# Attention plus mixer on one core: one token tile of two batches is kept and multiplied with the next batch's tile as a seven-product pair

## The chip, the cores and the metric

The kernel runs on one core of one Trainium2 chip. The metric is the device time of one execution in microseconds (us). Engines are named as in the profile: PE is TensorE (matrix products; PEld its weight loads), DVE is VectorE, ACT is ScalarE, POOL is GpSimd, and SP is the queue that issues most transfers.

## The reference, cut to what matters

Eight batches, 12 heads, 448 tokens, 64 elements a head:

```
scores = q @ k^T / sqrt(64) - log(448)
x  = sigmoid(scores) @ v               # per head, heads side by side: [8, 448, 768]
u  = x + (relu(x^T @ w_tok1) @ w_tok2)^T
out = u + relu(u @ w_ch1) @ w_ch2      # w_ch1 768 x 1536, w_ch2 1536 x 768
```

The last line is the part that the change touches: for each batch, `h2 = relu(u @ w_ch1)` has 448 tokens of 1536 values, and the output is `h2 @ w_ch2` plus `u`, in fp32.

## The kernel before, in words

The work is a pipeline written out by hand: each engine runs its instructions in the order of the program, and waits by semaphores. Token tiles of a batch are 0, 1 and 2 (128 tokens each) and a last one of 64.

Batches 3 to 7 run in `steady(b, u)`, three cycles (u = 0, 1, 2) a batch. A batch b brings 21 units of attention scores (`score`, L187 on PE, a sigmoid on ACT at L194), 6, 6 and 9 in the three cycles; `av` multiplies the sigmoids of the cycle before by v (L218), casts the result on DVE (L227) and sends it through a transposing transfer (`xtrans_dma`). `tok_tail` and `tok1` are the first product of the token mixer (L277, L296) with ReLUs on ACT (L310); `ytrans` is the second (L316), added to x on DVE (L326). After the second cycle's `ytrans` a copy (L339) and the transfer `un` (L343) put u of batch b - 1 into token order.

The third cycle ends with `sevens(b - 1)`, the product with w_ch1 for batch b - 1 by seven products in place of eight (Strassen's scheme in Winograd's form; L514), in the order "1ab 2a 2b 1c 6ab 5ab 2c 6c 5c 7ab 7c 3ab 4ab 3c 4c". ACT copies products 1, 6 and 5 out of PSUM into buffers `parts` (L535); DVE adds later ones to them (L544, L547). Its token sums (`token_sums`, L457) are made on DVE earlier in the third cycle.

The product with w_ch2, here called the output product, runs two batches behind: in batch b it is that of lot b - 2. Tiles 0 and 1 of the lot form a pair of rows for `ch2_seven`: seven products, numbered 1 to 7, each 6 matmuls of 384 columns, with weights that are sums of parts of the two tiles (`sums`, L801, DVE). The products accumulate on three chains: 1, 6, 7, 4 on bank X in this order, 2 on Y, 5 and 3 on Z (Y and Z are the same bank, one after the other). After each product, DVE adds what the bank holds to the output (L841), and the next product of that chain has to wait for this read. After products 3 and 4 the two tiles' outputs are stored (`store`, L621, two transfers on SP).

Two products can run side by side in quarters of the array (`two_jobs`, L861, six steps of four 64x64 matmuls in each of two halves). Between the halves stands `turn_over`, a copy of one column by DVE (L852, `turned`), for which PE waits. In cycle 0 the pair (1, 2) runs like this, then 6 and 5 as plain products (L814); in cycle 1 the pair (7, 3), then 4. The plain products stand between `tok1` and `ytrans`. Cycle 2 does the 64-token tile (`last_split`, L669) and then tile 2 alone: `ch2_pair`, 7 of 12 blocks in quarters (L387), the other 5 as 10 plain matmuls (L650) right before `sevens`, with an add on DVE for each half (L607).

Three copies of q and k into pair order for the next batch (`rel_k`, `rel_q`, L129) are made on DVE: one after cycle 0's `ytrans`, two in cycle 1 before `tok_tail`, three after cycle 1's `ytrans`; the transposing transfers `tr_k` and `tr_q` (L142) follow on SP. GpSimd issues the loads of later batches once `tr_q` has landed.

Buffers: output tiles 0 and 1 share a ring of four buffers, `parts`, with ACT's copies; a buffer is free again when its store has landed. Tile 2 has a buffer of its own (`outs`). `h2` has one buffer, `un` two.

Of the kernel before, what the change touches and what calls it, by code (L numbers as in the profile page):

```python
# [9 lines left out]
FP16 = mybir.dt.float16  # L10
FP32 = mybir.dt.float32
# [10 lines left out]
NJ = 7  # L22
NP = 64
NU = 3
# [6 lines left out]
def kernel(  # L31
# [11 lines left out]
    nc = tc.nc  # L43
# [6 lines left out]
    NCB = CC // 128  # L50
# [10 lines left out]
    pa = ctx.enter_context(tc.tile_pool(name="pa", bufs=2))  # L61
# [286 lines left out]
    h2 = {}  # L348
# [110 lines left out]
    def ch1_seven(b, banks):  # L459
# [300 lines left out]
    class ch2_seven:  # L760

        CHAIN = {1: "X", 6: "X", 7: "X", 4: "X", 2: "Y", 5: "Z", 3: "Z"}

        def __init__(self, rows, sides, X, Y, Z, at_end=True):
# [3 lines left out]
            hid = pa.tile(  # L768
                [128, 3, NCB // 2, 128], FP16, tag=tag, bufs=bufs, name=f"hid_{b}"
            )  # L770
            self.held = {n: hid[:, at, :, :] for at, n in enumerate((5, 6, 7))}
# [62 lines left out]
        def end(self, n):  # L834
            row, half = {1: (0, 0), 2: (0, 0), 6: (0, 1), 3: (0, 1)}.get(n, (1, int(n != 4)))
            b, t = self.rows[row]
            if (b, t) not in outs:
                out_tile(b, t)
            o = outs[b, t][:, DH * half : DH * half + DH].rearrange("s (u d) -> s u d", d=128)
            opens = n in (1, 6, 5, 4)  # L840
            nc.vector.tensor_tensor(  # L841
                out=o,
                in0=un[b][:, :, half, t, :] if opens else o,
                in1=self.ps[self.CHAIN[n]][:, 0:DH].rearrange("s (u d) -> s u d", d=128),
                op=ADD,
            )
            if n in (3, 4):
                store(b, t)

    def turn_over(ps):  # L850

        nc.vector.tensor_copy(out=turned[:, :], in_=ps[:, 0:1])  # L852
# [448 lines left out]
    def score(n=1):  # L1301
        for _ in range(n):
            qk(*next(scores))

    def steady(b, u):

        lot, before, ahead = b - 2, divmod(NU * b + u - 1, NU), divmod(NU * b + u - 2, NU)
# [2 lines left out]
        def run(steps, n):  # L1310
            for f in steps[:n]:
                f()
            del steps[:n]

        at_bank[0] = X
        if u < 2:
# [31 lines left out]
            at_bank[0] = Y  # L1348
            tok_tail(*ahead)
            tok1(*ahead, with_scores=True)  # L1350
            for n in ((6, 5), (4,))[u]:
                seven.plain(n)
        else:
            ps = [bank([128, 512], FP32, f"c2_{lot}_3_{r}") for r in range(2)]
            steps, end = last_split(lot, ps)
# [138 lines left out]
```

## Time and profile before

| what | us |
|---|---|
| median of three runs | 342.08 (341.51 to 342.49) |
| profiled execution, its own time | 341.39 |
| its span on the core | 339.6 |
| one batch of `steady` (each of 3 to 7) | 38.3 |
| PE busy | 332.2 (98%) |
| DVE busy | 234.9 (69%) |
| ACT busy | 213.0 (63%) |

How to read it: the columns of a timeline are start in us from the span's start, duration in us, engine, line of the kernel, operation, output and input, and a count; in square brackets stands the idle time before it and what ended that. Rows merge neighbours of one kind, and matmuls overlap, so the time that PE spends on some is read from the start of one row to the start of the next. The share of time that an engine is busy is an average over a batch whose three cycles differ.

### The profile page before, as it was taken

The page shows a single profiled execution, that of the slowest core. Times are in us where ns is not written, and L with a number is a line of the kernel's source. Part 1 is how long each engine was busy: PE and PEld are TensorE (multiplying, and loading weights), DVE is VectorE, ACT ScalarE, POOL GpSimd, SP SyncE. Part 2 cuts the span into 40 slices and gives each one's busy share as a digit, 9 for nine tenths or more (in the row PEclk, how much of TensorE's full clock was granted, in tenths as well). Part 3 has the DMA queues.
Part 4 walks back from the last instruction along what each step waited for, and adds up shares of the span by engine and source line. Part 5 has one row for each costly group of instructions (what it writes and reads, how often), then busy time and mean ns, then how long its engine had stood idle before and what let it go on. Part 6 is the DMA issues. An engine that isn't in the chain of part 4 may idle for free.

```text
span 339.6 us, 10285 instructions
## 1 busy us (share of the span) xinstructions
PE 332.2 (98%) x4423; PEld 242.5 (71%) x4423; DVE 234.9 (69%) x484; ACT 213.0 (63%) x272; POOL 58.7 (17%) x102
## 2 busy tenths in 40 slices
PE   7999999999999999999999999999999999999994
PEld 4555565555796679866896679866896679769852
DVE  2277366678998973877768773878758654876882
ACT  3997657388647895578647895578647795314200
POOL 8981550050031000220032002020010000000000
PEclk9999999999999999999999999999999999999999
DMA  7999999999999999998999899988995293028007
GB/s 119 173 174 195 206 205 204 163 175 237 169 187 189 140 168 211 185 142 161 204 145 172 138 206 175 206 117 134 196 175 93 56 193 73 2 56 185 4 11 197
DMA packets 104381, 52.17 MB, mean 154 GB/s; under 512 B 76432, under 2 KB 101264, under 8 KB 104336
## 3 DMA queue, kind: packets, MB, share of 16 engines
q1 hardware_dynamic: 78704, 29.11, 47.8%
q0 software_dynamic: 25168, 21.50, 42.1%
q10 hardware_dynamic: 464, 0.92, 1.0%
q8 instruction: 34, 0.56, 0.7%
q14 instruction: 11, 0.09, 0.1%
HBM read 43.45 MB, written 11.01 MB: 160 GB/s over the span
## 4 chain that ended last, share of the span: by engine, by line
PE 86%; DMA 5%; POOL 4%; ACT 2%; issue 1%; DVE 0%; ACTq 0%; POOLq 0%
PE c_ab L514 14%; PE c L814 10%; PE qk L187 9%; PE c_c L514 8%; PE xa L218 7%; PE c L861 6%; PE tk L296 5%; PE yt L316 5%; PE c L387 4%; DMA c<-in_moe_w_ch_dram 4%; PE c L584 4%; PE c L364 3%; PE c L669 3%; PE c L650 2%; ACT att L194 2%; DMA raw_v<-in_v_dram 2%
## 5 line engine op out<-in xcount | busy, mean ns | idle before, releaser
L194 ACT ACTIVATE att<-qk,att_bias 128x896 f16<-128x896 f32 x168 | 156.0, 1012 | 38.6 <-PE qk L187 37.6
L187 PE MATMUL qk<-tr_q,tr_k 64*64 64x448 f16 x672 | 61.3, 360 | 0.3 <-ACT att L194 0.2
L514 PEld LDWEIGHTS <-c 128*128 128x128 f16 x504 | 48.4, 98 | 1.1 <-issue 0.3
L218 PE MATMUL xa<-att,raw_v 64*64 64x448 f16 x644 | 40.7, 349 | 0.0
L187 PEld LDWEIGHTS <-tr_k 64*64 64x64 f16 x672 | 25.2, 105 | 19.0 <-issue 11.9
L514 PEld LDWEIGHTS <-sum 128*128 128x128 f16 x378 | 36.3, 98 | 0.0
L227 DVE CAST xu<-xa 128x448 f16<-128x448 f32 x40 | 23.1, 619 | 18.8 <-PE xa L218 18.4
L535 ACT ACTIVATE pt_ab<-c_ab 128x896 f32<-128x896 f32 x21 | 19.2, 917 | 20.6 <-PE c_ab L514 20.6
L218 PEld LDWEIGHTS <-raw_v 64*64 64x64 f16 x672 | 22.0, 107 | 8.3 <-issue 0.4
L861 PE MATMUL c<-c,h 64*64 64x384 f16 x360 | 24.6, 322 | 0.0
L1127 POOL COPY gate<-tr_q 128x2 f16<-128x2 f16 x6 | 1.6, 275 | 121.7 <-DMA tr_q<-rel_q 121.7
L326 DVE TENSOR_TENSOR xu<-xu,yt 128x448 f16<-128x448 f16 x38 | 21.7, 613 | 0.0
L537 ACT ACTIVATE h<-c_ab 128x896 f16<-128x896 f32 x7 | 6.4, 917 | 24.4 <-PE c_ab L514 24.4
L296 PE MATMUL tk<-xn,w 128*128 128x256 f16 x156 | 21.2, 274 | 0.1
L544 DVE TENSOR_TENSOR h<-pt_ab,c_ab 128x896 f16<-128x896 f32 x14 | 15.2, 1084 | 8.6 <-PE c_ab L514 8.6
L544 DVE TENSOR_TENSOR h<-pt_c,c_c 128x448 f16<-128x448 f32 x21 | 12.9, 614 | 11.7 <-PE c_c L514 11.6
L316 PE MATMUL yt<-w,h 128*128 128x448 f16 x88 | 20.3, 353 | 0.0
L841 DVE TENSOR_TENSOR o<-un,c 128x384 f32<-128x384 f16 x32 | 17.4, 550 | 4.0 <-PE c L814 4.0
L310 ACT ACTIVATE h<-tk 128x256 f16<-128x256 f32 x42 | 14.2, 406 | 9.5 <-PE tk L296 9.5
L814 PEld LDWEIGHTS <-hid 128*128 128x128 f16 x132 | 12.9, 98 | 8.0
L514 PE MATMUL c_ab<-diffs,c 128*128 128x224 f16 x168 | 18.4, 259 | 0.0
L296 PEld LDWEIGHTS <-w 128*128 128x128 f16 x156 | 13.6, 98 | 5.7 <-issue 2.4
(134 smaller groups left out, 572.1 us busy)
## 6 DMA issues: line engine op xcount, KB each, us to landing
out_dram<-o SPq DMA_DIRECT2D x41, 192.0 KB, 3.2
c<-in_moe_w_ch_dram POOLq DMA_DIRECT2D x4, 1152.0 KB, 16.1
raw_k<-in_k_dram POOLq DMA_DIRECT2D x10, 336.0 KB, 6.9
raw_q<-in_q_dram POOLq DMA_DIRECT2D x10, 336.0 KB, 5.7
raw_v<-in_v_dram POOLq DMA_DIRECT2D x10, 336.0 KB, 8.8
out_dram<-o SPq DMA_DIRECT2D x15, 96.0 KB, 2.4
raw_q<-in_q_dram POOLq DMA_DIRECT2D x12, 112.0 KB, 5.1
raw_k<-in_k_dram POOLq DMA_DIRECT2D x12, 112.0 KB, 5.4
```

Of the source, the lines that this page charges most:

```text
L187: nc.tensor.matmul(out=ps[64 * g : 64 * g + 64, hi, 0:S], lhsT=tr[b, "k"][64 * hi : 64 * hi + 64, u, j, 64 * g : 64 * g + 64], rhs=tr[b, " ...
L194: nc.scalar.activation(out=att[b, u, j][:, :, :], in_=ps[:, :, 0:S], func=SIGMOID, bias=bias_t[:, :], scale=att_scale,)
L218: nc.tensor.matmul(out=ps[g][64 * hi : 64 * hi + 64, 0:S], lhsT=raw[b, "v"][64 * g : 64 * g + 64, u, hi, j, :], rhs=att[b, u, j][64 * g : ...
L227: nc.vector.tensor_copy(out=xu(b)[:, u, g, 0:S], in_=ps[g][:, 0:S])
L296: nc.tensor.matmul(out=ps[tcb], lhsT=w1[rows, t, cols], rhs=xn[b, u][rows, :, t, :], start=(t == 0 and not with_scores), stop=(t == (2 if ...
L316: nc.tensor.matmul(out=ps[:, 0:S], lhsT=h1[b, u][:, tcb, g, :], rhs=w2[:, tcb, :, :], start=(tcb == 0), stop=(tcb == 1),)
L326: nc.vector.tensor_tensor(out=x, in0=x, in1=ps[:, 0:S], op=ADD)
L514: nc.tensor.matmul(out=ps[:, g, p, :], lhsT=weights[n][:, d, 128 * cb : 128 * cb + 128], rhs=moving[n][:, d, :], start=(n in (1, 5, 2) and ...
L535: nc.scalar.activation(out=shaped(part[:, :, :]), in_=ps, func=COPYF)
L544: nc.vector.tensor_tensor(out=shaped(dst), in0=shaped(parts[gs, which]), in1=ps, op=ADD)
L814: nc.tensor.matmul(out=ps[:, 0:DH], lhsT=self.weights[n][:, k, :], rhs=self.moving[n][:, k, :], start=(n in (1, 2, 5) and k == 0), stop=(k ...
L861: nc.tensor.matmul(out=ps[m : m + 64, 0:DH], lhsT=lhsT(n)[part, m : m + 64], rhs=rhs(n)[part, :], start=(opens and turn == 0 and n == 0), ...
```

## The change

In batches 4 and 6 tile 2 of the lot (lots 2 and 4) is not multiplied. Instead its `h2` columns are copied to a buffer `late` (which takes the place of `outs`) and its part of `un` to `un_late`, both on DVE. In the batch that follows (5 and 7) it forms a pair with tile 2 of the next lot (3 and 5), and seven products do both: (1, 2) in quarters, then 6, 5, 7, 3, 4 as plain products before `sevens`. The four sums of weights overwrite columns of `h2` that are no longer needed. The outputs of tile 2 of lots 2 to 5 now come from `parts`.

In batches 4 and 6 the products of the pair of tiles 0 and 1 are placed anew: (1, 2) and 6 in the first cycle, (5, 7) and no plain product in the second, (3, 4) in quarters at the start of the third. So both of their stores are issued in the third cycle. The order of `rel_k`, `rel_q` and the transfers around them is as before. Batch 3 and the end of the kernel are as before.

```diff
+    LATE_TILE = {4: 2, 6: 4}
+    PAIRED = {b + 1: lot for b, lot in LATE_TILE.items()}
+    un_late = {}
...
-        tag, bufs = ("outs", 1) if t == 2 else ("parts", 4)
+        late = b in LATE_TILE.values() or b - 1 in LATE_TILE.values()
+        tag, bufs = ("outs", 1) if t == 2 and not late else ("parts", 4)
...
+    def late_pair(lot):
+        free = h2[lot]
+        return ch2_seven(
+            [(PAIRED[lot + 2], 2), (lot, 2)],
+            [h2[PAIRED[lot + 2], "late"], free[:, :, 256:384]],
+            X,
+            X + 1,
+            X + 1,
+            at_end=False,
+            held={
+                5: free[:, LOW, 0:128],
+                6: free[:, HIGH, 0:128],
+                7: free[:, LOW, 128:256],
+                3: free[:, HIGH, 128:256],
+            },
+        )
...
-            turn0, turn, turn1, end = two_jobs([seven.job(n) for n in ((1, 2), (7, 3))[u]])
+            pair = ((1, 2), (5, 7) if b in LATE_TILE else (7, 3))[u]
+            turn0, turn, turn1, end = two_jobs([seven.job(n) for n in pair])
...
-            for n in ((6, 5), (4,))[u]:
+            for n in ((6,), ())[u] if b in LATE_TILE else ((6, 5), (4,))[u]:
                 seven.plain(n)
+        elif b in LATE_TILE:
+            turn0, turn, turn1, end = two_jobs([sevenfold[lot].job(n) for n in (3, 4)])
+            score(2)
+            run(turn0, 6)
+            turn()
+            at_bank[0] = Y
+            av(*before, 0, 2)
+            score()
+            run(turn1, 4)
+            score()
+            run(turn1, 2)
+            end()
+            av(*before, 2, 5)
+            score()
+            av(*before, 5, NJ)
+            xtrans_dma(*before)
+            at_bank[0] = X
+            ps = [bank([128, 512], FP32, f"c2_{lot}_3_{r}") for r in range(2)]
+            steps, end = last_split(lot, ps)
+            run(steps, 4)
+            score()
+            token_sums(b - 1)
+            run(steps, 3)
+            score()
+            run(steps, 3)
+            score()
+            run(steps, 2)
+            end()
+            late = pa.tile([128, NCB, 128], FP16, tag="outs", bufs=1, name=f"late_{lot}")
+            nc.vector.tensor_copy(out=late[:, :, :], in_=h2[lot][:, :, 256:384])
...
+            nc.vector.tensor_copy(out=un_late[lot][:, :, :, :], in_=un[lot][:, :, :, 2, :])
+            h2[lot, "late"] = late
+            at_bank[0] = Y
+            tok_tail(*ahead)
+            score()
+            tok1(*ahead, with_scores=True)
+            sevens(b - 1)
         else:
...
-            turn0, turn1, rest = ch2_pair(lot, u, 7, loose=True)
+            if b in PAIRED:
+                both = late_pair(lot)
+                turn0, turn, turn1, end = two_jobs([both.job(n) for n in (1, 2)])
+                rest = lambda: [both.plain(n) for n in (6, 5, 7, 3, 4)]
+            else:
+                turn0, turn1, rest = ch2_pair(lot, u, 7, loose=True)
+                turn, end = lambda: turn_over(turn_bank[0]), lambda: None
             run(turn0, 3)
             score()
             run(turn0, 4)
-            turn_over(turn_bank[0])
+            turn()
             av(*before, 5, NJ)
             xtrans_dma(*before)
             send()
+            if b in PAIRED:
+                both.sums(0, 2)
             token_sums(b - 1)
             score()
             run(turn1, 2)
             score()
             run(turn1, 5)
+            end()
+            if b in PAIRED:
+                both.sums(2, 4)
```

More of the change, by code (lines that the diff above doesn't have):

```diff
@@ L762, with __init__ @@
         CHAIN = {1: "X", 6: "X", 7: "X", 4: "X", 2: "Y", 5: "Z", 3: "Z"}
-        def __init__(self, rows, sides, X, Y, Z, at_end=True):
+        def __init__(self, rows, sides, X, Y, Z, at_end=True, held=None):
             self.rows, self.ps, self.banks = rows, {}, {"X": X, "Y": Y, "Z": Z}
@@ L767, in __init__ @@
             tag, bufs = ("tr_k", 2) if at_end else ("diffs", 1)
[L768 to L771, printed above, removed]
+            self.held = held
+            if not held:
+                hid = pa.tile(
+                    [128, 3, NCB // 2, 128], FP16, tag=tag, bufs=bufs, name=f"hid_{b}"
+                )
+                self.held = {n: hid[:, at, :, :] for at, n in enumerate((5, 6, 7))}
             if at_end:
@@ L840, in end @@
             opens = n in (1, 6, 5, 4)
+            u = un_late[b][:, :, half, :] if t == 2 and b in un_late else un[b][:, :, half, t, :]
             nc.vector.tensor_tensor(
                 out=o,
-                in0=un[b][:, :, half, t, :] if opens else o,
+                in0=u if opens else o,
                 in1=self.ps[self.CHAIN[n]][:, 0:DH].rearrange("s (u d) -> s u d", d=128),
@@ L1350, in steady @@
             tok1(*ahead, with_scores=True)
-            for n in ((6, 5), (4,))[u]:
+            for n in ((6,), ())[u] if b in LATE_TILE else ((6, 5), (4,))[u]:
                 seven.plain(n)
+        elif b in LATE_TILE:
[28 more added lines that the diff above has]
+            nc.vector.tensor_copy(out=late[:, :, :], in_=h2[lot][:, :, 256:384])
+            un_late[lot] = pa.tile(
+                [128, NU, 2, 128], FP16, tag="un_late", bufs=1, name=f"un_late_{lot}"
+            )
+            nc.vector.tensor_copy(out=un_late[lot][:, :, :, :], in_=un[lot][:, :, :, 2, :])
[5 more added lines that the diff above has]
+            sevens(b - 1)
         else:
```

1 line of the change is left out of this document (added).

## The prediction

> **What bounds the kernel now.** I read the busy shares, then busy time by batch, then the timelines of one batch on each engine. In the busy shares and in the stretches of batches 3 to 7 (columns: stretch, sum, TensorE, weight loads, VectorE, ScalarE, GpSimd, granted clock, DMA share, GB/s):
>
> ```profile
> PE 332.2 (98%) x4423; PEld 242.5 (71%) x4423; DVE 234.9 (69%) x484; ACT 213.0 (63%) x272; POOL 58.7 (17%) x102
> 140.48:178.79 38.31, 38.31 (x568) 30.11 (x564) 27.86 (x60) 26.87 (x35) 4.53 (x8) 1.00 0.98 168
> ```
>
> TensorE never pauses inside a batch, and all five batches take 38.3 us, so any TensorE time removed counts, unless another engine is then late. How late the others already are stands in the timelines of batch 4, TensorE first (start, duration; 6 matmuls of 384 columns start 0.163 us apart: 153.85 to 154.83):
>
> ```profile
> 153.85 1.14 PE L814 MATMUL c<-hsum_b,h 128*128 128x384 f16 x6
> 154.83 0.92 PE L316 MATMUL yt<-w,h 128*128 128x448 f16 x4
> 155.68 0.57 PE L187 MATMUL qk<-tr_q,tr_k 64*64 64x448 f16 x8
> ...
> 164.03 1.79 PE L650 MATMUL c<-c,h 128*128 128x384 f16 x10
> 165.66 1.31 PE L514 MATMUL c_ab<-xu,c 128*128 128x224 f16 x12
> ```
>
> The third cycle starts at 155.68, the channel products (L514) at 165.66. Around the end of the second cycle:
>
> ```profile
> 154.26 0.69 ACT L310 ACTIVATE h<-tk 128x256 f16<-128x256 f32 x2
> 155.00 0.30 PEld L316 LDWEIGHTS <-h 128*128 128x128 f16 x3 [0.18 <-ACT h L310]
> ```
>
> The second weight load of `yt` starts 0.05 us after ScalarE's second ReLU ends (154.95): ScalarE is already the last to arrive. VectorE in the third cycle:
>
> ```profile
> 155.50 1.14 DVE L326 TENSOR_TENSOR xu<-xu,yt 128x448 f16<-128x448 f16 x2
> 156.68 0.23 DVE L339 COPY xu<-xu 128x192 f16<-128x192 f16 x1
> 156.82 1.66 DVE L129 COPY rel_q<-raw_q 128x896 f16<-128x896 f16 x3
> ...
> 161.28 0.16 DVE L852 COPY turned<-c 128x1 f32<-128x1 f32 x1 [1.60 <-PE c L387]
> 161.51 1.16 DVE L227 CAST xu<-xa 128x448 f16<-128x448 f32 x2
> 162.81 0.92 DVE L457 TENSOR_TENSOR diffs<-xu 128x672 f16<-128x672 f16 x2
> ```
>
> It opens the cycle with 3 us of queued work and reaches `turned` (TensorE waits for it between the halves of a quad pair) idle; until 164.82 it does casts and token sums. The SP queue:
>
> ```profile
> 154.75 1.18 SPq L621 DMA_DIRECT2D out_dram<-o  x2
> 156.02 4.07 SPq L142 DMA_TRANSPOSE tr_k<-rel_k  x1
> 160.18 1.19 SPq L621 DMA_DIRECT2D out_dram<-o  x2
> 161.47 4.39 SPq L343 DMA_TRANSPOSE un<-xu  x1
> 165.99 3.17 SPq L142 DMA_TRANSPOSE tr_q<-rel_q  x1
> ```
>
> Each big transpose holds SP for 3 to 4.4 us; the second tile's store, ready at 155.6 (its last add on VectorE), went out at 160.18.
>
> **The change part by part.** Batches 4 and 6 keep, 5 and 7 pair. I work on batch 4's clock; batch 5's is 38.31 later. The products shrink by 6 matmuls a pair, 0.98 us; without any wait the two pairs would give -1.95.
>
> *Keeping batch, first cycle.* Product 5 goes: 6 x 0.163 = -0.98, in full, for the ReLUs there end at 146.76 and `yt` would start at 146.80. Its add (0.55 on VectorE) was hidden.
>
> *Second cycle.* Product 4 stood between `tok1` and `yt`, another -0.98. But `yt` now follows `tok1` at once and needs the ReLUs, queued behind six back-to-back sigmoids (148.90 to 154.26). Between 0 (ScalarE sets `yt`) and -0.98; the 0.05 us above says 0. So the third cycle starts 0.98 early, at 154.70.
>
> *Third cycle.* 14 quad steps and 10 plain matmuls go, 12 quad steps (products 3 and 4) come: -0.32 and -1.63. New is the place of `turned`: early in the cycle, behind the `yt` adds, L339 and three `rel_q` copies, which end at 158.48 - 0.98 = 157.50; with its 0.16 TensorE goes on at 157.72. TensorE gets there after 0.40 (two scores), 6 x 0.162, two `av` steps 0.38 and a score 0.19, at 156.64: a wait of 1.08, with everything behind it on TensorE. The split of the last tile reuses the banks that two adds must first read: 0.1 more. From 157.72 to the ninth score are 12 quad steps at 0.163, six at 0.163 of products 3 and 4, five `av` at 0.19, five scores at 0.19, `tok_tail` 0.15 and that 0.1: 5.1, so 162.8 against 163.0 before. ScalarE, idle during the wait, follows within 0.9 a score. Then 10 plain matmuls fewer: L514 starts at 163.83, -1.83 where the work alone says -3.90.
>
> *The two copies.* 1536 and 768 half-precision elements: 1.55 us by L129 (0.61 for 896), 1.1 by L547 (0.43 for 896); I take the copy row, 1.55. They end near 166.2, where VectorE's first combine is due at 167.96 - 1.83 = 166.1; the bank that this reads is needed again only 5.2 us after L514's start, 169.0. Cost nothing; without that cover 1.1 to 1.6.
>
> *Stores moved past transposes.* The stores of tiles 0 and 1 now both follow products 3 and 4, so on SP they come after `tr_k`, `un` and `tr_q`. From `rel_k` done (155.12 - 0.98, so 154.2): 4.07 + 4.39 + 3.17 and gaps of 0.1 make 166.1; the four halves go out 0.6 apart. Stores landed 3.1 to 4.4 us after issue in this stretch: tile 0 at 169.9 to 171.1, tile 1 at 171.0 to 172.3. Their buffers (`parts`) are those that ScalarE fills after channel products 6ab and 5ab; 6ab ends at 163.83 + 4.03 = 167.86 (before, those stores had landed 6 us earlier). ScalarE waits until about 170.5. TensorE meets it at 7ab and again at 7c, which comes 8.05 after L514's start and needs 6c's sums read: after tile 0's landing 1.2 to tile 1's, fills of 0.92 (5ab) and 0.55 (6c) and 0.1, so 173.3 instead of 171.9: 0.8 to 2.1, I take 1.4. `xn`, behind the stores, issues near 168.6 and is needed at 183. The loads that GpSimd gates on `tr_q` start some 3 us sooner. Keeping batch: -1.83 + 1.4 = -0.43.
>
> The Trainium skill ("DMA: Bandwidth & Descriptors", section "Issuing engines are not separate DMA queues") says that the time a sequencer spends on initiating a DMA is usually small relative to the DMA itself. Here `un` holds SP for 4.39 us of its 6.5 to landing, so the measurement decides; by the rule the stores would leave when their adds are done, this term would be 0, and the sum would be that of the second rival.
>
> *Pairing batch, third cycle.* Two quad steps fewer (-0.32), but the ninth score hangs on ScalarE's nine sigmoids (156.17 to 164.71, no gap), so 0.07 of it counts. `tok1` ends at 163.96. Five plain products, 30 matmuls, 4.88, stand where 10 (1.63) stood. Product 6 accumulates onto product 1's bank, which the first add must have read. On VectorE that add comes after `turned` (0.16 earlier, 161.12), the casts, two sums of 0.53 each and all four token sums: 164.82 + 1.05 - 0.16 = 165.7, read by 166.25. TensorE waits from 163.96 to 166.3: 2.35. Product 6 then 5 end at 168.25; product 7 needs the bank that product 6's add has read, behind the two later sums, at 168.5: 0.2 more. Product 4 ends at 171.42, against 165.66: +5.76 (work alone +2.93). Who waits: the channel products and all later.
>
> The paired tiles' buffers are awaited by 6ab and 6c. In batch 7 no loads run and the stores land in time. In batch 5, tile 2's store of before took 5.5 us beside the k and v loads, in batch 4 4.3; the kept tile's second half, on SP near 210.9, would land at 215.2 to 216.4. L514 starts at 209.3, 7c is due at 217.35 and waits for that landing, two fills of 0.92, one of 0.55 and 0.1: 0.4 to 1.6 late, 1.0.
>
> *Sum.* 2 x (5.76 - 0.43) + 1.0 = +11.7. The profiled execution took 341.39 (span 339.6), so 353.1; the median of the runs, 342.08, stands 0.69 above it: 353.7.
>
> **Rivals.** (1) *The work alone decides.* TensorE has been 98% busy and no row of before shows it waiting for VectorE in a batch: the time falls by 0.98 a pair, to 340.1. That holds if product 1's add is read by 163.96 and the other waits stay under a microsecond a pair. Against it: VectorE's rows fill 161.28 to 164.82 even without the two sums.
> (2) *The stores land in time.* If SP gives them out before `tr_q`, or its transposes are shorter with `un` issued sooner (the shortest of all was 3.64), nothing waits on `parts`: 2 x (5.76 - 1.83) = +7.9, 349.9. For it: the margin is 2 us in a chain of three transposes; against: SP issues in program order.
> (3) *The clock drops.* A pause of 2.35 us is longer than any wait of TensorE listed in this trace (1.2), and the granted clock is 1.00 in every batch. If it halved over the next three products, 18 x 0.163 = 2.9 a pair more: 359.6. The Trainium skill ("TensorE: Matmul & The Clock Gate", section "Why this matters for your kernels") warns of idle gaps above about 3 us; this one would stay under it, and no trace here shows a gap of that length.
> (4) *The stores land later still*, as batch 5's did (5.5) in both keeping batches: 2 x 1.1 and 0.6 more, 356.5.
>
> **How the numbers follow.** The forecast has 0.53, the work alone 0.05, stores in time 0.22, the clock 0.06, later stores 0.12; 0.02 is for a change under 0.3%. A measurement of this kernel tells about 0.3%, 1 us, from no change. Predicted 353.7; the range 349.3 to 357.0 takes in the forecast, in-time and later stores, 0.87, and leaves out the work alone, the clock and no change. Faster 0.05, within 0.3% 0.02, slower 0.93.
>
> **What would show it.** In the profile after: batches 4 and 6 near 37.9 us, batch 5 near 45, batch 7 near 44; TensorE's busy share near 94%; waits on TensorE for the add of `o` before the pair's product 6 (2.3 us, twice) and for `turned` in the keeping batches' third cycle (1.1, twice); weight loads of `yt` ended by the ReLU in the keeping batches' second cycle (0.9); ScalarE's `pt_ab` released by a store (2 to 3). I am wrong if product 6 starts right behind `tok1`, or if the keeping batches gain more than 2 us.

## The result, and the profile after

| | before | after |
|---|---|---|
| median of 6 runs each | 341.3 us (340.53 to 342.49) | 357.67 us (354.55 to 360.24) |
| profiled execution, its own time | 341.39 | 354.55 |
| its span | 339.6 | 352.8 |

The ratio is 1.0465 (95% interval 1.0431 to 1.05; it leaves out the slowest run, 360.24, which counts as slow): the change costs some 16 us by the medians and 13.2 us by the two profiled executions. The forecast was 353.7 with a range of 349.3 to 357.0, so the direction was right and the size too small. The profiled execution is the fastest of the runs of the changed kernel; what the others lost more is taken up below.

The busy shares of the changed kernel, and its busy time in batches 4, 5, 6 and 7 (columns as before: stretch, sum, TensorE, weight loads, VectorE, ScalarE, GpSimd, granted clock with 1.00 for full speed, DMA share, GB/s):

```profile
PE 333.2 (94%) x4387; PEld 239.1 (68%) x4387; DVE 243.7 (69%) x502; ACT 212.3 (60%) x272; POOL 58.1 (16%) x102
```

```profile
138.69:176.30 37.61, 35.41 (x536) 26.81 (x536) 27.75 (x60) 26.77 (x35) 4.58 (x8) 1.00 1.06 164
176.30:224.62 48.32, 43.47 (x579) 32.02 (x578) 32.17 (x68) 26.62 (x35) 4.52 (x8) 0.96 0.90 161
224.62:263.06 38.44, 35.40 (x535) 26.81 (x534) 27.67 (x59) 26.77 (x35) 3.20 (x6) 1.00 0.89 140
263.06:306.65 43.59, 41.52 (x579) 31.43 (x578) 28.75 (x62) 26.84 (x35) 0.00 (x0) 1.00 0.46 78
```

TensorE went from 98% to 94% with about the same busy time: 36 matmul records fewer, and pauses in every one of the four batches. Against 38.31 each, batch 4 gains 0.70, batch 5 loses 10.01, batch 6 loses 0.13 and batch 7 loses 5.28: together +14.7. The part ahead of batch 4 was 1.6 shorter (138.69 against 140.28; no instruction there was changed by the edit's text, and later runs gave 138.88 to 142.59), the rest differs by less than 0.1. So the loss lies in the pairing batches, and batch 5 loses twice what batch 7 does with the same instructions on TensorE. Batch 5 is also the only one of the four whose granted clock is not 1.00. Of the signs that the prediction named, batches 4 and 6 near 37.9 (38.0 on average), batch 7 near 44 (43.59) and the busy share near 94% came; batch 5, expected near 45, did not.

The waits of TensorE are in its timeline. The first two rows are of batch 4, the next three of batch 5, the last of batch 7 (in brackets the pause and what ended it):

```profile
152.17 1.02 PE L316 MATMUL yt<-w,h 128*128 128x448 f16 x4 [0.70 <-ACT h L310]
...
155.95 0.35 PE L869 MATMUL c<-hsum_b,h 64*64 64x384 f16 x2 [0.72 <-DVE turned L860]
...
202.25 3.27 PE L821 MATMUL c<-hsum_a,h 128*128 128x384 f16 x12 [2.28 <-DVE o L849]
...
208.80 1.31 PE L514 MATMUL c_ab<-xu,c 128*128 128x224 f16 x12
...
218.40 1.31 PE L514 MATMUL c_ab<-diffs,c 128*128 128x224 f16 x12 [2.54 <-ACT pt_ab L535]
...
288.81 2.11 PE L821 MATMUL c<-hsum_a,h 128*128 128x384 f16 x12 [2.07 <-DVE o L849]
```

The pauses that the forecast named are there: `yt` for the second ReLU, `turned` in the keeping batch, and product 6 of the pair for the first add of `o`, 2.28 and 2.07 us. What it did not have is in the durations. The first twelve matmuls after the pause took 3.27 in batch 5 and 2.11 in batch 7. From product 6 to L514 it is 208.80 - 202.25 = 6.55 in batch 5 and, in batch 7, whose L514 starts at 293.72, 4.91. The granted clock says why (busy time in four short stretches, the first three of batch 5, the last of batch 7):

```profile
202.20:204.00 1.80, 1.75 (x8) 0.94 (x8) 1.77 (x4) 0.00 (x0) 0.00 (x0) 0.73 1.01 182
204.00:206.00 2.00, 2.00 (x8) 0.96 (x7) 0.64 (x2) 0.00 (x0) 0.00 (x0) 0.50 1.16 216
206.00:208.00 2.00, 2.00 (x13) 1.14 (x12) 0.66 (x2) 0.00 (x0) 0.18 (x1) 0.89 1.07 197
288.80:291.00 2.20, 2.19 (x14) 1.30 (x14) 1.99 (x5) 0.00 (x0) 0.00 (x0) 1.00 0.34 69
```

After the pause of 2.28 the clock was 0.50 for about 3.4 us (in slices of 0.2 us it lies below 1.00 from 203.0 to 206.6, in the first and the last only in part); after the pause of 2.07, in this execution, it stayed at 1.00, and so it did after the pause of 2.54 further down.

The second thing in batch 5 is the pause of 2.54 at 7ab (218.40), behind a `pt_ab` that ScalarE could not write. ScalarE's timeline and SP's, both of batch 5, and then the transfers issued from 204 to 218 (KB each, median us from issue to landing):

```profile
217.43 1.73 ACT L535 ACTIVATE pt_ab<-c_ab 128x896 f32<-128x896 f32 x2 [5.01 <-DMA out_dram<-o]
```

```profile
197.47 4.75 SPq L343 DMA_TRANSPOSE un<-xu  x1
202.33 3.26 SPq L142 DMA_TRANSPOSE tr_q<-rel_q  x1
205.69 1.28 SPq L243 DMA_TRANSPOSE xn<-xu  x1
...
208.61 3.31 SPq L626 DMA_DIRECT2D out_dram<-o  x4
```

```profile
out_dram<-o SPq DMA_DIRECT2D x4, 192.0 KB, 7.7
raw_k<-in_k_dram POOLq DMA_DIRECT2D x2, 336.0 KB, 6.8
raw_v<-in_v_dram POOLq DMA_DIRECT2D x2, 336.0 KB, 10.4
```

The pair's four stores leave SP from 208.61 on, in the same moment as GpSimd's loads of `k` and `v` (from 208.25), and land 7.7 us after issue, where the stores of the keeping batches took 3.0 and 3.2.

### The profile page after: what moved, and what is told of

Read it like the earlier page. It is cut to its first block, busy times and chain, and to the rows that moved or that the text cites. A ratio compares the mean times of both kernels' runs of the same rounds, so it can differ in the third digit from the quotient of the medians.

```text
span 352.8 us, 10233 instructions
## 1 busy us (share of the span) xinstructions
PE 333.2 (94%) x4387; PEld 239.1 (68%) x4387; DVE 243.7 (69%) x502; ACT 212.3 (60%) x272; POOL 58.1 (16%) x102
## 4 chain that ended last, share of the span: by engine, by line
PE 74%; ACT 10%; DVE 6%; DMA 6%; issue 2%; SPq 0%; ACTq 0%; DVEq 0%
PE c L821 12%; PE c_ab L514 11%; ACT att L194 9%; PE qk L187 8%; PE xa L218 6%; PE c_c L514 6%; PE c L869 6%; PE yt L316 5%; DMA out_dram<-o 5%; PE tk L296 4%; PE c L589 3%; PE c L364 3%; PE c L674 2%; DMA first_q<-in_q_dram 1%; PE c L899 1%
## 5 line engine op out<-in xcount | busy, mean ns | idle before, releaser
L187 PE MATMUL qk<-tr_q,tr_k 64*64 64x448 f16 x672 | 59.3, 357 | 0.7 <-ACT att L194 0.2
L514 PEld LDWEIGHTS <-c 128*128 128x128 f16 x504 | 48.4, 98 | 6.3 <-issue 5.7
L514 PEld LDWEIGHTS <-sum 128*128 128x128 f16 x378 | 36.3, 98 | 0.0
L849 DVE TENSOR_TENSOR o<-un,c 128x384 f32<-128x384 f16 x36 | 19.7, 551 | 5.6 <-PE c L821 5.6
L821 PEld LDWEIGHTS <-h 128*128 128x128 f16 x120 | 12.2, 103 | 13.2 <-issue 6.5
L849 DVE TENSOR_TENSOR o<-o,c 128x384 f32<-128x384 f32 x30 | 16.3, 552 | 7.0 <-PE c L821 3.7
L514 PE MATMUL c_ab<-diffs,c 128*128 128x224 f16 x168 | 18.4, 259 | 2.5 <-ACT pt_ab L535 2.5
```

Of the source, the lines that this page charges most:

```text
L187: nc.tensor.matmul(out=ps[64 * g : 64 * g + 64, hi, 0:S], lhsT=tr[b, "k"][64 * hi : 64 * hi + 64, u, j, 64 * g : 64 * g + 64], rhs=tr[b, " ...
L514: nc.tensor.matmul(out=ps[:, g, p, :], lhsT=weights[n][:, d, 128 * cb : 128 * cb + 128], rhs=moving[n][:, d, :], start=(n in (1, 5, 2) and ...
L821: nc.tensor.matmul(out=ps[:, 0:DH], lhsT=self.weights[n][:, k, :], rhs=self.moving[n][:, k, :], start=(n in (1, 2, 5) and k == 0), stop=(k ...
L849: nc.vector.tensor_tensor(out=o, in0=u if opens else o, in1=self.ps[self.CHAIN[n]][:, 0:DH].rearrange("s (u d) -> s u d", d=128), op=ADD,)
```

## The experiments

All kernels start from the changed one; their edits are shown cut. Their batches, read from the first scores of one to the first scores of the next, in us of the profiled execution:

| kernel | batch 4 | 5 | 6 | 7 | median of runs |
|---|---|---|---|---|---|
| before | 38.30 | 38.31 | 38.31 | 38.31 | 341.3 |
| after | 37.61 | 48.32 | 38.44 | 43.59 | 357.67 |
| idle matmuls in the pause | 37.59 | 46.70 | 38.02 | 43.58 | 354.1 |
| token sums split | 37.79 | 49.24 | 37.63 | 41.66 | 354.45 |
| transposes behind stores, batches 4 and 6 | 36.76 | 47.35 | 36.76 | 43.59 | 352.01 |
| loads of batch 5 later | 37.46 | 45.44 | 37.56 | 43.58 | 352.06 |
| these three edits together | 36.77 | 49.81 | 36.77 | 41.66 | 353.12 |
| and `rel_q` behind `turned` | 35.86 | 49.34 | 35.86 | 41.66 | 351.11 |
| instead `yt` behind `turned` | 36.05 | 48.10 | 36.06 | 41.66 | 350.69 |
| second pair alone | 38.31 | 38.31 | 38.55 | 45.21 | 348.65 |
| batch 5's transposes and loads behind its stores | 35.86 | 41.87 | 35.85 | 41.66 | 343.05 |
| the same, second pair alone | 38.30 | 38.31 | 35.85 | 41.66 | 342.08 |

**Is the clock part of it?** The pause is kept and filled with matmuls whose result nobody reads, so that TensorE is busy and product 6 still starts when the add is done.

```diff
-                rest = lambda: [both.plain(n) for n in (6, 5, 7, 3, 4)]
+                def rest():
+                    idle = two_banks(f"idle_{b}")[0]
+                    for _ in range(20):
+                        nc.tensor.matmul(out=idle[:, 0:256], lhsT=c2[:, 0, 0:128],
+                                         rhs=c2[:, 0, 0:256], start=True, stop=True)
+                    for n in (6, 5, 7, 3, 4):
+                        both.plain(n)
```

> The changed kernel with 20 idle matmuls of 256 columns (about 2.2 us of TensorE) put right before the pair's product 6 in batches 5 and 7, where TensorE waits 2.28 and 2.07 us for product 1's add; nothing else moves. Theory clock: the pauses let the granted clock fall to a half afterwards (0.50 from 204 to 206 us in the profiled run, 18 matmuls 0.32 instead of 0.163 us apart), in more of the pauses in the slower runs, whose mean clock is 0.986 to 0.990 against 0.995; with the pauses filled the clock is 0.998 or more in every run, the runs lie within 1.5 us of each other, and the median falls from 357.7 to 353 to 355. Theory transfers: what makes the runs differ is when stores land; then the median stays at 357 to 358 and the runs spread over 3 us or more.

Measured: 354.1 us (353.44 to 355.96), ratio 1.0382 (1.0332 to 1.0433), 3.6 us under the changed kernel by the medians; the runs spread over 2.5 us and not 1.5. TensorE's timeline in batch 5, with the added matmuls, and a stretch behind them:

```profile
200.49 2.35 PE L1438 MATMUL idle<-c 128*128 128x256 f16 x20
202.94 2.11 PE L821 MATMUL c<-hsum_a,h 128*128 128x384 f16 x12
```

```profile
204.50:206.50 2.00, 2.00 (x14) 1.17 (x12) 1.33 (x3) 0.00 (x0) 0.00 (x0) 1.00 1.72 143
```

The twelve matmuls take 2.11 again, the clock stays at 1.00 (mean of the runs 0.995 to 1.0; of the changed kernel's runs near the median 0.989 to 0.990), and from product 6 to L514 it is 207.85 - 202.94 = 4.91, as in batch 7. So the halved clock is shown, at 1.64 us for one event (6.55 - 4.91). That more work in the pause saves time is the plainest sign of it. Between the two profiled executions batch 5 gains 1.62 and batch 7, which had kept its clock, nothing (43.58 against 43.59).

**Is product 6's wait the add's place behind the token sums?** VectorE's timeline of the changed kernel in batch 5 shows the four token sums (L457) and then the add (L849) that product 6, started at 202.25, waited for:

```profile
199.73 0.92 DVE L457 TENSOR_TENSOR diffs<-xu 128x672 f16<-128x672 f16 x2
200.68 0.51 DVE L457 TENSOR_TENSOR diffs<-diffs,xu 128x672 f16<-128x672 f16 x1
201.22 0.51 DVE L457 TENSOR_TENSOR diffs<-xu,diffs 128x672 f16<-128x672 f16 x1
201.65 0.55 DVE L849 TENSOR_TENSOR o<-un_late,c 128x384 f32<-128x384 f16 x1
```

The edit does two token sums well ahead of the add and two behind the pair's products:

```diff
-    def token_sums(b):
+    def token_sums(b, first=0, last=4):
...
             send = end(put_off=True)
+            if b in PAIRED:
+                token_sums(b - 1, 0, 2)
...
-            token_sums(b - 1)
+            else:
+                token_sums(b - 1)
...
             rest()
+            if b in PAIRED:
+                token_sums(b - 1, 2, 4)
             sevens(b - 1)
```

> The changed kernel with the token sums of batches 5 and 7 taken out of the way of product 1's add: the first two come right after the 64-token tile's adds, where VectorE idles 1.4 us, the last two after the pair's product 4. Theory VectorE order: product 6 starts 0.4 to 0.6 us after tok1 instead of 2.1 to 2.3, the clock stays at 0.998, and batch 5 and 7 lose 1.6 us each and one to two halved stretches of 1.7 less: 357.7 falls to 351 to 353. Rival: the sums of weights themselves (L808) hold product 6, or the wait only moves to product 7; then the time falls by less than 1 us apart from the clock, to 354 to 356.

Measured: 354.45 (354.13 to 356.03), ratio 1.0393 (1.0348 to 1.0438), where 351 to 353 was expected. The wait is nearly gone (0.36), and batch 7 falls from 43.59 to 41.66 as expected. Batch 5 does not fall, it rises. Its TensorE rows:

```profile
201.55 2.11 PE L822 MATMUL c<-hsum_a,h 128*128 128x384 f16 x12 [0.36 <-DVE o L850]
...
216.50 2.17 PE L515 MATMUL c_ab<-diffs,c 128*128 128x224 f16 x12 [2.97 <-ACT pt_ab L536]
...
220.28 1.28 PE L515 MATMUL c_c<-diffs,c 128*128 128x224 f16 x6 [1.61 <-ACT pt_c L536]
```

The products end sooner (L515 starts 3.55 earlier in the batch than L514 did), but the stores leave SP no sooner: at 210.01, 32.50 after the batch's first scores, against 32.31. The pause comes back at 7ab and 7c, with the halved clock behind it (12 matmuls in 2.17 where 1.31 is the usual time), and for twice as long: in slices the clock lies below 1.00 from 216.6 to 223.6. The two costs of batch 5 stand one behind the other: taking the first away pays into the second.

**Do the stores of the keeping batches wait behind SP's transposes?** In the changed kernel SP gives out `tr_k`, `un` and `tr_q` one after the other and then the stores (batch 4):

```profile
152.71 3.17 SPq L142 DMA_TRANSPOSE tr_k<-rel_k  x1
155.93 3.85 SPq L343 DMA_TRANSPOSE un<-xu  x1
159.88 3.91 SPq L142 DMA_TRANSPOSE tr_q<-rel_q  x1
163.89 2.47 SPq L626 DMA_DIRECT2D out_dram<-o  x4
```

The edit issues `un` and `tr_q` after products 3 and 4, in batches 4 and 6:

```diff
             run(turn1, 2)
             end()
+            utrans(b - 1, copy=False)
+            some(1)
+            gated_loads(b)
             av(*before, 2, 5)
...
+        stores_first = u == 1 and b in LATE_TILE
         if u == 1:
-            utrans(b - 1)
-        some(behind)
-        if u == 1 and b < B - 1:
+            utrans(b - 1, send=not stores_first)
+        some(behind - stores_first)
+        if u == 1 and b < B - 1 and not stores_first:
             gated_loads(b)
```

> The changed kernel with un and tr_q of batches 4 and 6 issued on SP after the stores of tiles 0 and 1, and not ahead of them (the GpSimd loads that wait for tr_q so start some 4 us later). Theory stores: ScalarE's fills after 6ab and 5ab no longer wait for a store, 7ab and 7c follow without a pause, and the keeping batches are 0.8 and 1.7 us shorter: 357.7 falls to 354.7 to 355.7. Rival: the pause at 7c has another cause (ScalarE's queue behind nine sigmoids); then the time stays within 1 us of 357.7, and ScalarE still pauses before 6ab's fill.

Measured: 352.01 (351.23 to 354.07), ratio 1.0333 (1.0277 to 1.0388), better than expected. SP's rows of batch 4 now:

```profile
152.90 3.19 SPq L142 DMA_TRANSPOSE tr_k<-rel_k  x1
158.14 2.40 SPq L628 DMA_DIRECT2D out_dram<-o  x4
160.58 4.98 SPq L345 DMA_TRANSPOSE un<-xu  x1
```

The stores leave 5.75 us sooner, no `pt_ab` waits for one in batches 4 and 6, and these fall by 0.85 and 1.68, both to 36.76. What one execution shows by batch (3.5 together with 0.97 in batch 5) is less than the 5.7 by the medians. The mean clocks of the runs (0.990 to 0.995 here, 0.986 to 0.995 for the changed kernel) suggest that the clock dropped less often here; no trace of the other runs shows it.

**Does batch 5's store wait come from the loads beside it?** The loads are gated on a later value:

```diff
             sevens(b - 1)
+            if b == 5:
+                nc.gpsimd.tensor_copy(out=gate[:, :], in_=h2[b - 1][:, 0, 0:2])
+                gated_loads(b)
...
-        if u == 1 and b < B - 1:
+        if u == 1 and b < B - 1 and b != 5:
             gated_loads(b)
```

> The changed kernel with batch 5's k and v loads (1344 KB) held until the first part of h2 of that batch is made, about 4 us later, so that they run behind the paired tiles' stores and not beside them. Theory contention: those stores, which took 7.7 us to land beside the loads, land in 3 to 4 us, 6ab's fill waits under 1 us instead of 5.0, TensorE's pause of 2.54 us before 7ab is gone: 357.7 falls to 354.5 to 355.5. Rival: the stores are late because product 3 and 4 end late and SP issues them late (209 to 212 us); then landing gets faster but the pause stays above 1.5 us and the time falls by less than 1 us.

Measured: 352.06 (351.1 to 352.81), ratio 1.0312 (1.0269 to 1.0356), better than expected. The transfers of batch 5 in this kernel (205 to 220), and TensorE's row:

```profile
out_dram<-o SPq DMA_DIRECT2D x4, 192.0 KB, 2.8
```

```profile
203.00 3.50 PE L821 MATMUL c<-hsum_a,h 128*128 128x384 f16 x12 [2.28 <-DVE o L849]
```

The stores land in 2.8 instead of 7.7 us, the channel products run without a pause, and batch 5 falls from 48.32 to 45.44. The wait for the add and the halved clock stay, as they should. So the long landing time of these stores comes from the loads that share the DMA engines with them: k and v now start at 213.70, 4.3 us behind the first store (209.36), and in the changed kernel they started at 208.25, beside it (208.61).

**The three together.** Edits 2, 3 and 4 in one kernel.

> The changed kernel with three causes taken away together: token sums of the pairing batches split around product 1's add, un and tr_q of the keeping batches issued after the stores, batch 5's loads held back. Theory (the loss is these three waits and the halved clock that two of them bring): keeping batches 36.8 us each, as when the stores went first; pairing batches 38.31 + 3.3 = 41.6, from batch 7 of the run with split sums; clock 0.997 or more; four batches 156.8 against 153.2, so 3.6 above before: 344 to 345.5. Rival (a wait taken away comes back elsewhere, as the split sums did at the store of batch 5): batch 5 stays above 43 us and the time is 347 or more.

Measured: 353.12 (352.1 to 353.29), ratio 1.0376 (1.0348 to 1.0405): some 8 us more than expected. Batches 4, 6 and 7 came as expected (36.77, 36.77, 41.66); batch 5 took 49.81, with the clock below 1.00 from 216.0 to 223.0. SP's rows there, and TensorE's at 7ab:

```profile
196.77 4.63 SPq L345 DMA_TRANSPOSE un<-xu  x1
201.51 3.26 SPq L142 DMA_TRANSPOSE tr_q<-rel_q  x1
...
208.42 2.48 SPq L629 DMA_DIRECT2D out_dram<-o  x4
```

```profile
215.00 1.42 PE L517 MATMUL c_ab<-diffs,c 128*128 128x224 f16 x12 [3.20 <-ACT pt_ab L538]
```

L514 (L517 in this kernel) starts at 204.74, 4.1 us sooner than in the changed one (3.6 counted from the batch's first scores), but SP gives out the stores at 208.42, no sooner than before (208.61): it is now SP's own queue, `un`, `tr_q` and `xn`, that they stand behind. And the later gate has moved forward with the work, so the loads go out at 209.03, beside them again. Two causes feed the same wait, and each run so far had removed one.

**Two more waits in the keeping batches.** First `rel_q`'s copies behind `turned`, on top of the three edits:

```diff
             turn()
+            some(3)
             at_bank[0] = Y
             av(*before, 0, 2)
...
-        some(behind - stores_first)
+        some(0 if stores_first else behind)
```

> As the run with three causes mended, and in the keeping batches the three rel_q copies come after turned and not before it. Theory VectorE queue: the pause of 0.7 us at turned goes, and the channel products start 0.7 to 0.9 earlier in each keeping batch, 1.4 to 1.8 less than the run with three mended. Rival (the nine sigmoids bound the third cycle anyway): under 0.3 us less in each keeping batch.

Measured: 351.11 (350.02 to 352.15), ratio 1.0315 (1.028 to 1.035). Batches 4 and 6 fall from 36.77 to 35.86, which is the price of the wait for `turned`: 0.91 a batch. Batch 5 stays high, at 49.34, with pauses of 3.69 and 0.59 and behind them the clock (busy time in that stretch):

```profile
215.20:222.20 7.00, 6.10 (x33) 4.63 (x33) 2.52 (x5) 2.04 (x4) 0.00 (x0) 0.51 0.91 163
```

Then, in place of that order, the `yt` of the second cycle is moved behind `turned` as well, so that TensorE need not wait for the ReLU:

```diff
             turn()
             at_bank[0] = Y
-            av(*before, 0, 2)
+            ytrans(*divmod(NU * b + u - 3, NU))
+            utrans(b - 1, send=False)
+            some(3)
             score()
...
+            at_bank[0] = Y
+            av(*before, 0, 5)
             score()
...
+        if u == 1 and b in LATE_TILE:
+            return
         at_bank[0] = Y
         ytrans(*ahead)
```

> As the run with three causes mended, and in the keeping batches yt of the second cycle stands behind the third cycle's first two scores and half of the quad steps, with L339 and rel_q behind turned. Theory ReLU: yt no longer waits for ScalarE (0.98 us gained), turned comes at once (0.7 to 0.9 gained), two more changes between quarter and full matmuls cost 0.3: each keeping batch 1.3 to 1.6 shorter than with three mended, 35.3, and the time 341 to 342.5, level with before. Rival (ScalarE's nine sigmoids and the ReLUs ahead of them bound the third cycle): the ninth score moves by less than 0.5, and the time stays above 343.

Measured: 350.69 (349.75 to 351.32), ratio 1.0301 (1.0272 to 1.033), 8 to 10 us over what was expected, since batch 5 (48.10) had the same store wait as in the run before (1.53 at 7ab, 2.72 at 7c, and a halved clock behind it). In the keeping batches nothing was won over the run before either, 36.05 against 35.86: the pause of 0.7 at `yt` went, and one of 0.63 for the add of `o` came ahead of the last tile's split.

**The second pair alone.** One line, and the kernel has no pair in batch 5:

```diff
-    LATE_TILE = {4: 2, 6: 4}
+    LATE_TILE = {6: 4}
```

> The change for the second pair alone (batch 6 keeps, batch 7 pairs; batches 4 and 5 as before). In the profiled run batch 6 was +0.1 and batch 7 +5.3, without a halved clock. Theory: the loss is local to each pair, so +5.4, and up to 1.7 more where the pause in batch 7 halves the clock: 346 to 348.5. Rival (the loss lies mostly in the first pair's meeting with the loads and does not exist without it): below 344; or the pairs disturb each other: above 349.

Measured: 348.65 (346.7 to 351.04), ratio 1.0247 (1.019 to 1.0303), just over the 346 to 348.5 expected. Here the pause of 2.07 us in batch 7, which left the clock alone in the changed kernel, halved it (TensorE's row, and busy time in the stretch):

```profile
283.50 3.66 PE L821 MATMUL c<-hsum_a,h 128*128 128x384 f16 x12 [2.07 <-DVE o L849]
```

```profile
283.50:287.20 3.70, 3.70 (x13) 1.80 (x13) 2.02 (x5) 0.00 (x0) 0.00 (x0) 0.55 0.25 53
```

Product 6 to L514 is 290.05 - 283.50 = 6.55 again, batch 7 is 45.21 instead of 43.59. The same pause at the same place costs 0 in one execution and 1.64 in another. The four runs follow their mean clock only in part: 346.7 at 0.998, 347.73 at 0.994, 349.57 at 0.995, 351.04 at 0.989. The last is the profiled one, and it has a second drop far ahead of the pair, from 34.6 to 38.2, behind a pause of 2.68 for the load of a weight; its batch 4 starts at 142.59, 2.3 later than before. So a mean clock does not say where the clock dropped.

**Batch 5's stores ahead of its transposes and loads.** On top of the run with `rel_q` behind `turned`, `tr_q`, `un` and the loads of batch 5 are given out after the pair's products:

```diff
             sevens(b - 1)
-            if b == 5:
-                nc.gpsimd.tensor_copy(out=gate[:, :], in_=h2[b - 1][:, 0, 0:2])
+            if b in PAIRED and b < B - 1:
+                utrans(b - 1, copy=False)
                 gated_loads(b)
...
+        pairing = u == 1 and b in PAIRED and b < B - 1
         if u == 1:
-            utrans(b - 1, send=not stores_first)
-        some(0 if stores_first else behind)
-        if u == 1 and b < B - 1 and not stores_first and b != 5:
+            utrans(b - 1, send=not (stores_first or pairing))
+        some(0 if stores_first else behind - pairing)
+        if u == 1 and b < B - 1 and not (stores_first or pairing):
             gated_loads(b)
```

> The run before this one in the series (all sums split, queue order mended in the keeping batches, rel_q behind `turned`) has batches of 35.86, 49.34, 35.86 and 41.66 us; all that is still lost lies in batch 5, whose last four stores leave SP at 208.48, behind `un` (4.57 us), `tr_q` (3.27) and `xn`, and land beside the k and v loads (7ab waits 3.69, 7c 0.59). Here batch 5's `tr_q`, `un` and its loads are given out behind its stores. Theory (the stores' place in SP's queue and the loads beside them are the whole rest): batch 5 comes to batch 7's 41.7 to 42.5, no wait at L517 over 0.5, the span falls by 7 to 7.7, 343 to 344.5 us; the four batches then sum to 155.0 to 155.9, against 153.2 in the kernel before, so still slower by 1.8 to 2.7 less what the opening gains (1 to 1.6). Rival (the pair in batch 5 is long for another cause, the moved transposes come late for batch 6's first scores or its product 1, or the clock): batch 5 over 45 or batch 6 over 37, 347 us or more.

Measured: 343.05 (342.26 to 343.34), ratio 1.0044 (1.0023 to 1.0064), as expected. SP's rows in batch 5, and the busy time by batch:

```profile
204.07 3.25 SPq L629 DMA_DIRECT2D out_dram<-o  x4
207.42 3.84 SPq L142 DMA_TRANSPOSE tr_q<-rel_q  x1
211.31 3.77 SPq L345 DMA_TRANSPOSE un<-xu  x1
```

```profile
139.46:175.32 35.86, 35.05 (x535) 26.62 (x534) 27.51 (x59) 26.82 (x35) 4.33 (x8) 1.00 0.99 162
175.32:217.19 41.87, 41.52 (x578) 31.85 (x577) 32.33 (x69) 26.84 (x35) 4.80 (x9) 1.00 0.92 163
217.19:253.04 35.85, 35.04 (x535) 26.61 (x534) 27.37 (x60) 26.81 (x35) 3.20 (x6) 1.00 1.10 175
253.04:294.70 41.66, 41.51 (x577) 31.44 (x576) 28.83 (x63) 26.85 (x35) 0.00 (x0) 1.00 0.55 93
```

The stores leave at 204.07 in place of 208.48, batch 5 falls from 49.34 to 41.87, batch 6 pays nothing for the later transposes, and the clock is 1.00 in all four. The 7.47 that batch 5 gains are, to within 0.2, the two pauses of the run with `rel_q` behind `turned` (3.69 + 0.59) and half speed over 6.10 us of TensorE's work (3.0). The run moves the stores ahead of the transposes and of the loads at once, so how much of it belongs to SP's queue and how much to the loads is not shown. With this, 14.6 of the 16.4 us by the medians are accounted for by edits that touch only the order of VectorE's, SP's and GpSimd's queues. The four batches sum to 155.24 against 153.23.

**The same with the second pair alone**, to see whether seven products for two tiles pay once these waits are gone (`yt` still waits 0.71 for the ReLU):

```diff
-    LATE_TILE = {4: 2, 6: 4}
+    LATE_TILE = {6: 4}
```

> The second pair alone (tile 2 of lot 4 kept in batch 6 and done in batch 7) with the same mends. Theory (what is left when no wait is left is the difference of work: 35.86 + 41.66 = 77.5 against two batches of 38.31 = 76.6): batches 4 and 5 at 38.3 as in the kernel before, 6 at 35.9, 7 at 41.7; 340.9 to 342.5 us, level with the kernel before within its spread. Rival (the waits taken away hid something that comes out when only one pair is made, or the keeping itself costs more than its batch shows): 343.5 or more. Rival on the other side (seven products for eight pay once the waits are gone): under 340.

Measured: 342.08 (341.54 to 343.56), ratio 1.0023 (1.0002 to 1.0044). Batches 6 and 7 take 35.85 + 41.66 = 77.51 against 76.62: 0.9 more, where the medians (341.19 for before in this comparison) say 0.9. None of these kernels beats the one before.

## Why the prediction was too low

The terms of its sum, with what the profiled execution of the changed kernel measured:

| term | predicted | measured |
|---|---|---|
| batches 4 and 6, up to L514 | -1.83 each | -1.53, -1.54 |
| batches 4 and 6, wait for stores behind L514 | +1.4 each | +0.84, +1.68 |
| batch 5, third cycle up to L514 | +5.76 | +7.12 |
| batch 7, third cycle up to L514 | +5.76 | +5.27 |
| batch 5, wait for stores behind L514 | +1.0 | +2.90 |
| sum | +11.7 | +14.7 |

From 353.7 to 357.67 it is 3.97: +3.1 in these terms, -1.6 for the opening ahead of batch 4, which no term had and which by luck hid a part of the miss, and +2.4 since the median stands 3.1 and not 0.69 above the profiled execution. The miss in the terms lies in batch 5, 1.36 ahead of L514 and 1.90 behind it; the others are off by up to 0.6 each and by -0.2 together.

*Right in place, and nearly in size.* The third cycle of batches 4 and 6 starts 0.98 early, as worked out: product 5 counts in full and product 4 not at all, for `yt` waits for the ReLU (0.70). `turned` holds TensorE for 0.72 by the row and 0.91 by the run that took the wait away (1.08 and 0.1 predicted). The stores go out behind `tr_q`, as predicted: the three transposes held SP for 3.17 + 3.85 + 3.91 = 10.93 in place of 11.63, so 163.89 stands against 164.5 (the predicted 166.1 less the 1.59 by which this batch starts sooner). The wait they cause averages 1.26 in place of 1.4. That these batches gained 1.53 up to L514 and not 1.83 lies behind `turned`: from there to the ninth score it is 5.60 (155.95 to 161.55) where 5.1 was added up. Product 6 waits 2.28 and 2.07 for the add behind the four token sums (2.35 predicted). Product 7 did not wait (0.2 predicted): in batch 7 it starts 1.99 after product 6, without a pause. Moving two token sums away brought batch 7 to 41.66, +3.35, where the work alone says 2.93; of the difference 0.31 is what is left of the wait at product 6, which starts 0.97 behind `tok1` where L650 started 0.66 behind it. The two copies cost nothing, being hidden; they took 0.55 and 0.36 us, 0.91 in place of the 1.55 taken and under the lower bound of 1.1 as well, without effect on the sum.

*The step that failed first: the clock, put at nothing in the sum and kept as a rival with 0.06.* The prediction saw that a pause of 2.35 was longer than any listed before, priced a halving at 2.9 a pair, and then gave it next to no chance because no row of before showed one. The price was too high and the chance far too low: one halving costs 1.64 from product 6 to L514, and it came in batch 5 of the profiled execution, in batch 7 of another kernel, and after pauses at 7ab. Filling the pauses of 2.1 to 2.3 us gave back 3.6 us of the median, to 354.1. That this is the forecast to within 0.4 is partly luck: batch 5's stores cost 2.91 in that kernel, too, and its opening was 0.9 shorter than before. How far a pause decides it, the kept traces show: in batches 4 to 7 of all twelve, TensorE pauses 14 times for 2 us or more. Within about 1 us of the end of eight of these pauses (2.07 to 3.69 us) the clock halved, after five (2.07 to 2.54) it did not, and one fell into a drop that was running; without such a pause just before it the clock never halved in these batches. A drop lasted 3.6 us in slices, in three kernels 7.0. What the trace of before offered was no evidence that the clock holds through such a pause, only that it had not been tried; the fitting treatment was a term with both ends, 0 and 2 x 2.9, and not a rival to be left out of the range. The Trainium skill ("TensorE: Matmul & The Clock Gate", section "Why this matters for your kernels") warns of gaps above about 3 us; by that rule nothing would have happened here, and the runs differ: 2.28 and 2.07 were enough. The same page's section "What's actually happening" describes two clock states and an activity window of some 3.4 us that runs free of the kernel, and the trace agrees with that part: the granted clock falls to 0.50, for about 3.4 us or twice that, and the same pause of 2.07 drops it in one execution and not in another.

*The second: batch 5's term of 1.0 for the stores.* It took the 5.5 us that a store of before needed beside loads and added it to a later issue time. But the change puts four stores and 1.3 MB of loads on the DMA engines within the same 3.7 us (208.25 to 211.92), and the landing took 7.7 us; the wait came at 7ab (2.54) and not only at 7c. The landing time was read from a neighbour that met the loads at another moment. The runs show the loads as the cause: with them out of the way 2.8 us to landing and no wait. Once the products ended sooner, the stores stood behind `un`, `tr_q` and `xn` on SP and met the loads again, and the wait went only when the stores were put ahead of both. To the prediction's remark on SP, where the Trainium skill ("DMA: Bandwidth & Descriptors", section "Issuing engines are not separate DMA queues") calls the time for initiating a DMA usually small: the measurement decided there, and did so again here, for `un` held SP 3.77 to 4.98 us, and a change of the order on that queue (and of the loads behind it) moved batch 6 by 1.68.

*A third, in the median.* The forecast added 0.69 for the median over the profiled execution, from three runs; with six, the median of before is 341.3, 0.09 below its profiled execution. The profiled execution of the changed kernel turned out the fastest of its runs and the median 3.1 above it. Its mean clock is 0.995, which is the one drop (a mean of 0.53 from 203.0 to 206.6, so 1.7 us of clock lost, 0.0048 of 353); that of the three runs at 357.6 to 357.8 is 0.989 to 0.990, which is the size of a second one. The remaining 1.4 or so is not settled: one run at 0.994 took 357.03. The opening is a candidate, since 138.69 is the earliest start of batch 4 in the twelve traces (138.88 to 142.59 in the others), but the traces of those runs are not there to be read.

*Why the change does not pay even without its waits.* By the count of matmuls each pair of batches should have saved 0.98. With all of this mended a keeping batch gains 2.45 where the work alone says 3.90, and a pairing batch loses 3.35 where it says 2.93: together +0.90 and not -0.98. The difference in the keeping batch stands in two places: at `yt`, whose 0.98 comes to nothing because the ReLU is behind six sigmoids, and in the third cycle, where 1.46 of 1.95 arrives (153.88 to 162.40 in the last mended kernel with two pairs, 8.52, against 9.98). ScalarE, paced by the scores, sets the first; that it also sets the second was only argued, and the trace lists no wait of TensorE in that stretch.

## What to carry to other kernels

On a TensorE that never waits, a pause of two microseconds or more can cost more than itself: price it with the clock behind it, at both ends, even when no earlier trace shows a drop. A store's landing time belongs to the moment in which it is issued, so when a change moves stores, write down what else is on the same issuing queue and on the DMA engines at that moment. And when one wait is removed in a batch that has two, look at the second before counting the gain: here three correct mends together won nothing in batch 5 until a fourth was found.

## What the runs showed of the hardware that was not expected

- A pause of TensorE of 2.07 to 3.69 us can halve the granted clock (0.50 in the slice, matmuls of 384 columns 0.32 apart instead of 0.163) for about 3.4 us, worth 1.64 us here, or for twice that; the same pause does so in some executions only.
- Twenty matmuls with no use, 2.35 us in a pause that was there anyway, saved 3.6 us by the medians; in the profiled execution it was 1.62, in the one batch where the clock had dropped.
- Four stores of 192 KB took 2.8 to 4.0 us (median) to land where the loads started 2 us or more behind the first of them or not at all, and 4.8 to 7.7 in batch 5 of the seven kernels where 1.3 MB of loads were issued beside them.
